# Window attention and a sticky mixture of experts: the last eviction of an arm behind the switch, eight raw weight buffers, routing lists at two steps per chunk

## The chip, the cores and the metric

The kernel runs on one core of a Trainium2 chip. Five engines work side by side, each through its own queue in order: TensorE (PE in the profile, its weight loads PEld), VectorE (DVE), ScalarE (ACT), GpSimd (POOL) and SyncE (SP), which issues most DMAs. The metric is the device time in microseconds; the median of several runs counts.

## What is computed

Attention with a window of 32 to each side and 32 global tokens, over 8 batches and 8 heads, gives 576 rows of 512 numbers per batch, 4608 rows in all. Each row is then given to one of eight experts: the expert of its largest logit, or, where a second gate says so, the expert of the row before.

```python
for b in range(B):
    prev_e = -1
    for s in range(S):
        fresh_e = int(np.argmax(logits[b, s]))
        if s == 0 or local_gate[b, s] < 0.5:
            e = fresh_e
        else:
            e = prev_e if prev_e >= 0 else fresh_e
        prev_e = e
        ...
        h = np.maximum(x[b, s] @ w1[e], 0.0)
        out[b, s] = p[e] * (h @ w2[e])
```

All products of the experts are made in three passes, on a high and a low part of each operand: high by high, low by high, high by low.

## The kernel before

**Attention first, then blocks of experts.** `Attn.run` works off 48 units of attention. Behind them come the blocks of `Moe.run`, each with the weights of one expert. Blocks 0 to 2 are *early* ones of 256 rows, taken from the first five batches alone, and the rest of the attention and of the routing is threaded between their matmuls. Blocks 3 to 10 are one per expert (*rem* in the code): what is left of its rows, at most 512, in one of ten arms of a `Switch`, by their number. Behind them stand up to 14 *full* blocks of 256 rows, each within an `If`; with these inputs three of them run.

**Within a block.** `mm1` multiplies by the first weight: eight steps (`fc`) of 12 matmuls; ACT takes the relu out of PSUM as the high part (`hh`), DVE the low part (`hl`). In the program's names the parts of later blocks lie in tiles called `wp` and `wq`. `mm2` multiplies by the second weight for one group of 128 rows: eight steps of three matmuls into one PSUM bank. `store` evicts that bank on ACT, scaled by the gate (`y`), and POOL scatters `y` to the output by an indirect DMA. POOL also gathers the rows of coming blocks (`gather`, into `xr` and `xa`), and `xpose` turns them on PE, ACT and DVE.

**The arms.** `arm` chooses: case 0 (`half`), which has only a group of 128 rows (group 2) and turns its relu on PE; case 1 (group 3 alone beside it); cases 2 to 9, `part`, with groups 0, 1 and, over 384 rows, 3. Behind the switch `close` does group 2 for every arm; ahead of that PE, ACT and the others load the next condition (`cnd`) and give a hint for the next switch (`hint`). Instructions behind a switch that depend on an engine's work within an arm wait for the end of that engine's arm, because the ten arms are merged there.

**Weights.** SP loads 512 KB pieces into `raw`, four buffers used in turn. `split` casts a piece on ACT to its high part; `flush` lets DVE subtract it for the low part, and only then issues the next load into that buffer. Split pieces lie in a ring of nine, so that about one block is split ahead. When a split stands in the program is written out: `SP` for the early blocks, `step` for the others.

**Routing lists.** Each `hook`, one per `fc` in the early blocks, advances the generator `tail` by one `yield`. `tail` ends the attention, ranks the rows, and runs `lists`: `place` counts, `low` builds one-hot tiles (`o`), and `pick` forms its operands on DVE in `xT` and then sums on PE, in 34 small matmuls, the row numbers `idx` that the first rem block gathers by. `kinds` computes the conditions `cnd` of the switches. `rest` picks the remaining lists, in twelve larger steps and 34 matmuls more. In `early`, block 2 forces what is not yet done: `finish(True)` at the first step of its second group runs `tail` up to `LISTS` and issues the gathers, and the hint for the first switch follows.

Of the kernel before, what the change touches and what calls it, by code (L numbers as in the profile page):

```python
# [37 lines left out]
GCH = [1, 4, 7, 10, 13, 14]  # L38
NX = 3
LISTS = "lists"  # L40
HEAVY = "heavy"
NF = (B * S) // 256
NR = NF - NX - 1
# [55 lines left out]
class Attn:  # L99
# [422 lines left out]
    def tail(self, sg, sl, fin, rt, moe):  # L522
        b = B - 1
        fin = [x for x in fin if x[0] is not None]
        self.g_t(sg)
        yield
        self.g_av(sg)
        self.at2.close()
        moe.alloc_a()
        yield  # L530
        self.l_t(sl, 0)
        self.l_t(sl, 1)
        yield
        self.l_av(sl, 0)
        yield
        self.l_av(sl, 1)
        self.at1.close()
        moe.alloc_b()
        yield
        while fin:  # L540
            f, a = fin.pop(0)
            f(*a)
            yield
        self.f1g(b)
        yield
        self.f1(b, 3)
        yield
        self.f2g(b)
        yield
        self.f2(b)  # L550
        yield from lag(2)
        self.f3(b, rt, False)
        yield
        c = self.cur[b]
        yield from every(rt.keys(b, c["L"]), 2)
        yield
        yield from rt.stage_b(self.ps_t, self.ps_o, rt.probs(b, c["L"], c["xa"]))
        self.f4(b, rt)
        yield from rt.lists(self.ps_o)
        yield LISTS  # L560
        yield from every(rt.rest(self.ps_o), RE)


# [23 lines left out]
class Route:  # L587
# [414 lines left out]
    def lists(self, po):  # L1002
# [28 lines left out]
            yield from self.low(c0, min(c0 + 5, NT))  # L1031
        self.pk = (cid, phi)
        yield from self.pick(cid, phi, self.o2, 0, 4, 2 * NX, ((0, NT),), po)
        yield from self.kinds()
        nc.vector.tensor_scalar(out=self.eid[:, 0:NR], in0=self.ek[0:1], scalar1=float(E - 1), scalar2=None, op0=ALU.min)
        yield
        nc.vector.tensor_tensor(out=self.eoh[:, NX + E:NSLOT], in0=ge[:, :, 0:E], in1=ge[:, :, 1:E + 1], op=ALU.subtract)
        yield

    def kinds(self):  # L1040
        nc = self.nc
        nc.vector.tensor_scalar(out=self.cnd[:, 0:1], in0=self.lim[0:1, E - 1:E], scalar1=0.5, scalar2=float(-E), op0=ALU.mult, op1=ALU.add)
        yield
        q = self.tmp("kq", [1, E], I32)
# [23 lines left out]
class Moe:  # L1068
    def __init__(self, tc, cst, rt, xs, buf, raw, ps, w1, w2, out):
# [15 lines left out]
        self.xt0 = None  # L1085
        self.go = False
        self.got = False
        self.cv = {}
        self.tail = None
        self.raws, self.wp, self.pend, self.nld, self.ex = [], [], [], 0, {}  # L1090
# [153 lines left out]
    def hook(self, i, k):  # L1244
        if self.tail is not None:
            try:
                if next(self.tail) == LISTS:
                    self.go = True
            except StopIteration:
                self.tail = None  # L1250
        self.flush()
        if i == NX - 1:
            self.finish()
        for _ in range(SP[i][k]):
            self.split()

    def finish(self, force=False):
        while force and not self.go:
            self.go = next(self.tail) == LISTS
        if self.go and not self.got:  # L1260
            self.gather(NX)
            self.got = True
# [10 lines left out]
    def early(self, i):  # L1273
# [9 lines left out]
        for fc in range(8):  # L1283
            self.mm2(i, py, fc, 0, *x[2:])
            self.hook(i, 8 + fc)
            if not mid and fc in (1, 3):
                self.xpose(i + 1, fc // 2)
                if fc == 3 and i + 2 < NX:
                    self.gather(i + 2)
        self.store(py, 0)  # L1290
        py = self.py()
        if mid:
            self.widen()
        for fc in range(8):
            if mid and fc == 0:
                self.finish(True)
                self.hint(i + 1)
            self.mm2(i, py, fc, 1, *x[2:])
            self.hook(i, 16 + fc)
            if mid and fc in XPM:  # L1300
                self.xpose(i + 1, XPM.index(fc))
        self.store(py, 1)
        if mid:
            all_(self.tail or ())
            self.tail = None
            self.gather(i + 2)
            self.ph.t.append(self.ps[6])
            self.py.t.append(self.ps[7])

    def half(self, i):  # L1310
        nc = self.nc
        XH, XL, HH, HL = self.XH, self.XL, self.HH, self.HL
        hr = []
        js = slice(P * REM, P * REM + P)

        def turn(k):
            tp = self.xtp().rearrange("p (t k) -> p t k", k=P)[:, 0:2]
# [24 lines left out]

    def part(self, i, n0, n1, groups):
        x = self.XH, self.XL, self.HH, self.HL
        for fc in range(8):
            self.mm1(i, fc, *x, n0, n1)
            self.step(fc % 2 == 0)
        for g, j in enumerate(groups):
            py = self.py()
            for fc in range(8):  # L1350
                self.mm2(i, py, fc, j, *x[2:])
                if g == 0:
                    self.step(fc in (1, 4))
                    if fc in (2, 5):
                        self.xpose(i + 1, fc // 3)
            self.store(py, j)

    def close(self, i, j):
        py = self.py()
        for fc in range(8):  # L1360
            self.mm2(i, py, fc, j, self.HH, self.HL)
            self.step(fc in (1, 4))
# [6 lines left out]
    def arm(self, i, case):  # L1369
        if case == 0:  # L1370
            self.half(i)
        elif case == 1:
            self.part(i, 256, 512, [3])
        else:
            n = 256 + GRAIN * (case - 1)
            self.part(i, 0, n, [0, 1] + [3] * (n > 384))

    def bound(self, k, most):
        if k not in self.cv:
# [52 lines left out]
def kernel(ctx: ExitStack, tc: tile.TileContext, qk, qg, vw, wgl, wgg, w1, w2, out):  # L1432
# [17 lines left out]
    moe.hr = Ring([at.gsb[:, 0:256], at.gsb[:, 256:512]])  # L1450
    w = 2 * (2 * E + NR)
    rt.o2 = at.xT.rearrange("p a b -> p (a b)").bitcast(BF16)[:, 0:NT * 2 * w].rearrange("p (t a w) -> p t a w", a=2, w=w)
    moe.xr += [at.xa.t[0][:, k] for k in range(2)]
    at.at1, at.at2 = s1, s2
    at.run(rt, moe)
# [57 lines left out]
```

## Time and profile before

| | us |
|---|---|
| runs | 727.65, 728.07, 733.19 |
| median | 728.07 |
| profiled execution | 730.23 |
| its span, first to last instruction | 728.5 |
| attention with the first early block begun | 0 to about 255 |
| first arm starts | 331.91 |
| short arm (`half`) of the second rem block | 378 to 393 |
| first full block | 639.53 |
| last instruction on PE ends | 709.8 |

A group's row gives engine, line, busy time and count, and then the idle time just before its instructions with what ended it. In a timeline a number in brackets is the idle time before the row and behind the arrow what ended it; "issue" stands where the profile shows no releaser. The granted clock of PE was 0.974 on average.

### The profile page before, as it was taken

How to read it: one execution, taken by the hardware profiler on the slowest of the kernel's cores; microseconds unless marked ns; L12 is line 12 of the kernel's file. 1: busy time of each engine (PE TensorE's matmuls, PEld its weight loads, DVE VectorE, ACT ScalarE, POOL GpSimd, SP SyncE). 2: the span in 40 equal slices, each digit the busy share in tenths (PEclk: the TensorE clock that was granted, in tenths of full speed). 3: DMA queues.
4: the chain of work that ended last, by engine and by line, in shares of the span. 5: the costliest groups of instructions: out<-in, count | busy, mean ns of one | idle time of the engine just before them, and what ended most of it. 6: DMA issues, size and time to landing. Idle time of an engine off the chain costs nothing.

```text
span 728.5 us, 18458 instructions
## 1 busy us (share of the span) xinstructions
PE 678.0 (93%) x7253; PEld 562.8 (77%) x7253; DVE 435.5 (60%) x1141; ACT 344.8 (47%) x613; POOL 194.0 (27%) x320
## 2 busy tenths in 40 slices
PE   8999999999899899979996999989899999999990
PEld 6777777777667869958884979878788879799880
DVE  7878778778787777974427444335444425165560
ACT  4555555554445646623344534244444425255550
POOL 7534434434143110122042112140303030112210
PEclk9999999999999999989997999999999999999995
DMA  8866786866584677863437635445555533367762
GB/s 337 351 249 238 305 292 247 317 251 241 186 315 163 209 239 236 278 227 107 161 116 250 193 125 188 145 152 183 163 176 170 160 105 116 118 211 239 233 203 92
DMA packets 42789, 150.93 MB, mean 207 GB/s; under 512 B 7869, under 2 KB 9149, under 8 KB 38464
## 3 DMA queue, kind: packets, MB, share of 16 engines
q1 hardware_dynamic: 35392, 126.39, 50.1%
q0 software_dynamic: 6880, 21.90, 8.8%
q8 instruction: 77, 1.26, 0.7%
q14 instruction: 152, 1.25, 0.5%
q10 hardware_dynamic: 288, 0.13, 0.1%
HBM read 130.02 MB, written 19.42 MB: 205 GB/s over the span
## 4 chain that ended last, share of the span: by engine, by line
PE 31%; issue 20%; DVE 5%; POOL 3%; DMA 3%; ACT 1%; POOLq 0%; SPq 0%; ACTq 0%; DVEq 0%
PE ps L1233 15%; PE ps L1222 12%; DMA raw<-in_w_dram 2%; DVE wp L1148 2%; PE ps L1187 2%; POOL out_dram L1239 2%; POOL xr L1173 1%; PE ps L1330 1%; DVE wq L1148 1%; DMA xr<-xs,idx 1%; ACT y L1238 0%; DVE hl L1225 0%; ACT wp L1139 0%; DVE o L902 0%; DVE wp L1190 0%
## 5 line engine op out<-in xcount | busy, mean ns | idle before, releaser
L1233 PE MATMUL ps<-wp,wq 128*128 128x512 f32 x504 | 129.7, 404 | 4.6 <-ACT y L1238 3.2
L1148 DVE TENSOR_TENSOR wp<-raw,wp 128x1024 fp32r<-128x1024 f32 x79 | 95.6, 1219 | 61.4 <-ACT wp L1139 61.4
L1239 POOL DMA_INDIRECT out_dram<-y,tk x38 | 39.3, 1034 | 307.7 <-ACT y L1238 295.1
L1233 PEld LDWEIGHTS ps<-wp,wq 128*128 128x128 f32 x504 | 93.4, 190 | 26.5 <-ACT y L1238 4.9
L1222 PE MATMUL ps<-wp,wp 128*128 128x256 f32 (+5 forms) x672 | 109.7, 323 | 2.3 <-issue 2.3
L1222 PEld LDWEIGHTS ps<-wp,wp 128*128 128x128 f32 x672 | 103.5, 188 | 8.0 <-issue 3.0
L1139 ACT CAST wp<-raw 128x1024 fp32r<-128x1024 f32 x81 | 84.7, 1046 | 26.6 <-PE ps L1187 9.2
L1225 DVE SCALAR_TENSOR_TENSOR wq<-ps,wq 128x256 fp32r<-128x256 f32 (+5 forms) x80 | 41.6, 526 | 90.4 <-ACT wq L1224 81.0
L1224 ACT ACTIVATE wq<-ps 128x256 fp32r<-128x256 f32 (+5 forms) x80 | 37.1, 468 | 85.2 <-PE ps L1222 81.3
L190 POOL TENSOR_SCALAR_AFFINE_SELECT qbd<-raw 64x512 f32<-64x512 f32 x62 | 44.6, 720 | 120.4 <-PE ps L242 102.2
L242 PE MATMUL ps<-kx,qbd 128*64 128x128 f32 x1024 | 71.0, 279 | 2.9 <-issue 2.1
L242 PEld LDWEIGHTS ps<-kx,qbd 128*64 128x64 f32 x1024 | 54.7, 136 | 12.7 <-issue 7.4
L1238 ACT ACTIVATE y<-ps,pp 128x512 f32<-128x512 f32 x38 | 26.2, 688 | 76.2 <-PE ps L1233 73.9
L247 DVE TENSOR_REDUCE mx<-ps 128x4 f32<-128x512 f32 x64 | 43.9, 686 | 29.5 <-PE ps L242 29.3
L1173 POOL DMA_INDIRECT xr<-xs,idx x32 | 39.6, 1237 | 70.9 <-DVE L L390 17.5
L253 ACT ACTIVATE pe<-pe 128x512 f32<-128x512 f32 x64 | 40.7, 636 | 33.1 <-DVE pe L249 33.1
L249 DVE TENSOR_TENSOR pe<-ps,mx 128x512 f32<-128x512 f32 x64 | 44.0, 688 | 1.6
L275 PE MATMUL ps<-v,pt 128*32 128x65 f32 x2048 | 42.7, 222 | 2.0 <-DVE xa L283 0.8
L275 PEld LDWEIGHTS ps<-v,pt 128*32 128x32 f32 x2048 | 33.3, 110 | 13.8 <-issue 6.7
L190 POOL TENSOR_SCALAR_AFFINE_SELECT kx<-raw 128x384 f32<-128x384 f32 (+3 forms) x127 | 43.0, 372 | 3.4 <-DMA raw<-in_qk_dram 1.2
L261 ACT COPY pt<-ps 128x512 f32<-128x512 f32 x64 | 34.9, 610 | 16.5 <-PE ps L259 16.4
L1189 ACT CAST wp<-ps 128x512 fp32r<-128x512 f32 x40 | 23.4, 587 | 34.8 <-PE ps L1187 27.9
(270 smaller groups left out, 1117.9 us busy)
## 6 DMA issues: line engine op xcount, KB each, us to landing
raw<-in_w_dram SPq DMA_DIRECT2D x123, 512.0 KB, 3.5
v<-in_vw_dram SPq DMA_DIRECT2D x32, 1040.0 KB, 9.9
raw<-in_qk_dram SPq DMA_DIRECT2D x32, 528.0 KB, 6.3
xs<-xa SPq DMA_DIRECT2D x8, 1056.0 KB
qgb<-in_qg_dram SPq DMA_DIRECT2D x8, 128.0 KB, 3.2
out_dram<-y,tk POOLq DMA_INDIRECT x38, 2.7
xs<-xg SPq DMA_DIRECT2D x32, 16.0 KB, 4.1
xr<-xs,idx POOLq DMA_INDIRECT x32, 6.2
```

What stands on the lines that cost most here:

```text
L190: self.nc.gpsimd.affine_select(out=out, in_=in_, pattern=pat, compare_op=ALU.is_ge, fill=0.0, base=0, channel_multiplier=0)
L242: nc.tensor.matmul(sp[64 * t2:64 * t2 + 64, t], qbd[:, w], kf[:, f:f + P], start=False, stop=True, skip_group_check=True)
L247: nc.vector.tensor_reduce(out=mx, in_=st["sp"], axis=AX.X, op=ALU.max)
L249: nc.vector.tensor_tensor(out=st["pe"][:, 4 * hb:4 * hb + 4], in0=st["sp"], in1=mx.broadcast_to([P, 4, P]), op=ALU.subtract)
L275: nc.tensor.matmul(o[32 * w4:32 * w4 + 32, g, h], pt[:, 2 * g + w4 // 2, w4 % 2, h, :], v[:, w, h * (D + 1):(h + 1) * (D + 1)], start=True ...
L1139: nc.scalar.copy(out=hi, in_=raw)
L1148: (nc.gpsimd if pool else nc.vector).tensor_tensor(out=lo, in0=raw, in1=hi.bitcast(F32), op=ALU.subtract)
L1173: self.nc.gpsimd.indirect_dma_start(out=self.xr[j], out_offset=None, in_=src, in_offset=bass.IndirectOffsetOnAxis(ap=self.rt.idx[:, c0 + j ...
L1222: nc.tensor.matmul(ph, a[:, dc, fs], b_[:, dc, n0:n1], start=(n == 0), stop=(n == 11))
L1225: nc.vector.scalar_tensor_tensor(out=hl[:, fc, n0:n1], in0=ph, scalar=0.0, in1=hh[:, fc, n0:n1].bitcast(F32), op0=ALU.max, op1=ALU.subtract)
L1233: nc.tensor.matmul(py, a[:, fc, js], b_[:, fs], start=(fc == 0 and k == 0), stop=(fc == 7 and k == 2))
L1239: sc = nc.gpsimd.indirect_dma_start(out=self.out, out_offset=bass.IndirectOffsetOnAxis(ap=self.g[1][:, j:j + 1], axis=0), in_=y, in_offset ...
```

## The change

It has three parts.

1. *Eviction.* In the arms of a rem block the last group now goes to the PSUM bank `ps[7]`, and its `store` stands at the start of `close`, behind the switch, with the column 1 of the gates and row numbers. Over 384 rows the groups go in the order 3, 0, 1 instead of 0, 1, 3. Case 1 copies column 3 to column 1. `half`, which has no such group, sets the row numbers of column 1 to `1 << 20`, which the scatter drops. The other groups use banks 0 and 1 by number.
2. *Raw buffers.* After block 2 the ring `raw` takes four more buffers, in `xa` and `xT` of the attention, and four loads for them are issued at once.
3. *Lists.* `tail` now yields at every second step of `lists` and every third of `kinds`, which is a generator by itself with a mark `KINDS` behind it. In block 2 the gathers, if still missing, are issued before the first `store`; what is left of `kinds` is forced at the fifth step of the second group, and the first hint follows at its seventh.

```diff
@@ tail
-        yield from rt.lists(self.ps_o)
+        yield from every(rt.lists(self.ps_o), 2)
         yield LISTS
+        yield from every(rt.kinds(), 3)
+        yield KINDS
         yield from every(rt.rest(self.ps_o), RE)
@@ early
+        if mid:
+            self.widen()
+            self.finish(True)
         self.store(py, 0)
         py = self.py()
-        if mid:
-            self.widen()
         for fc in range(8):
-            if mid and fc == 0:
-                self.finish(True)
+            if mid and fc == 4:
+                while not self.known:
+                    self.take(next(self.tail))
+            if mid and fc == 6:
                 self.hint(i + 1)
...
+            self.py.k = 0
+            old = [self.raw() for _ in range(4)]
+            self.raw.t, self.raw.k = self.more + old, 0
+            for _ in self.more:
+                self.load()
@@ half
+        nc.vector.memset(self.g[1][:, 1:2], 1 << 20)
@@ part
         for g, j in enumerate(groups):
-            py = self.py()
+            last = j == groups[-1] and self.kind(i) == "rem"
+            py = self.ps[7] if last else self.py.t[g]
...
-            self.store(py, j)
+            if not last:
+                self.store(py, j)
@@ close
-        py = self.py()
+        py = self.py.t[j % 2]
+        if self.kind(i) == "rem":
+            self.store(self.ps[7], 1)
@@ arm
-            self.part(i, 0, n, [0, 1] + [3] * (n > 384))
+            self.part(i, 0, n, [3] * (n > 384) + [0, 1])
```

How this stands in the engines' queues, at the places that the prediction speaks of. First ACT at the end of the last arm and behind it; before, with `y2` as the eviction of the arm's last group from bank `ps7`:

```order
L1238 ACTIVATE y0_4316<-ps0_63,pp0_92 128x512
L1238 ACTIVATE y1_4317<-ps1_64,pp0_92 128x512
L1238 ACTIVATE y2_4318<-ps7_70,pp0_92 128x512
L1508 UNCONDITIONAL_BRANCH
L1380 TENSOR_LOAD cnd_296
L1386 SWITCH_STRIDE
L1386 ISA
L1386 BRANCH_PREFETCH_HINT
L1139 CAST wp6_4312<-raw1_78 128x1024
```

and now:

```order
L1242 ACTIVATE y0_4316<-ps0_63,pp0_92 128x512
L1242 ACTIVATE y1_4317<-ps1_64,pp0_92 128x512
L1532 UNCONDITIONAL_BRANCH
L1403 TENSOR_LOAD cnd_296
L1409 SWITCH_STRIDE
L1409 ISA
L1409 BRANCH_PREFETCH_HINT
L1242 ACTIVATE y2_4318<-ps7_70,pp0_92 128x512
L1143 CAST wp6_4312<-xT_112 128x1024
```

The eviction of `ps7` moved behind the branch, and the cast reads one of the new raw buffers.

PE around the 34 matmuls of the first `pick` (only its end is shown; `o1` and `xT` are its operands). Before, it stands in the first group of block 2 (bank `ps0`, weights `wq1`):

```order
L996 LDWEIGHTS o1_290
L996 MATMUL ps6_69<-xT_112,o1_290 128x8
L1233 MATMUL ps0_63<-wq1_4315,hh_90 128x512 x2
L1233 MATMUL ps0_63<-wq1_4315,hl_91 128x512
L1233 MATMUL ps0_63<-wq1_4315,hh_90 128x512 x2
```

and now in the second group of block 1 (bank `ps1`, with five of the eight steps still to come):

```order
L999 LDWEIGHTS o1_290
L999 MATMUL ps6_69<-xT_112,o1_290 128x8
L1237 MATMUL ps1_64<-wp1_101,hh_90 128x512 x2
L1237 MATMUL ps1_64<-wp1_101,hl_91 128x512
L1237 MATMUL ps1_64<-wp2_4207,hh_90 128x512 x2
```

`pick` moved up by 18 steps: five of that group, the eight of `mm1` and five of the first group of block 2.

DVE where the operands of that `pick` (`xT`) are made. Before, among the steps `hl` of block 2:

```order
L902 TENSOR_TENSOR o1_290<-io128_261,plo_289 128x384
L1225 SCALAR_TENSOR_TENSOR hl_91<-ps2_65,hh_90 128x256
L986 TENSOR_TENSOR xT_112<-cid_4745,phi_3669 128x34x4
L1148 TENSOR_TENSOR wp2_4207<-raw2_79,wp2_4207 128x1024
L1225 SCALAR_TENSOR_TENSOR hl_91<-ps3_66,hh_90 128x256
L988 TENSOR_TENSOR xT_112<-xT_112,t1_264 128x34x4
L990 TENSOR_SCALAR xT_112<-xT_112,ipf_266 128x34x4
```

and now ahead of all of them, between splits of weights that block 2 uses (`wq0`), the second of which is the one that starts at 295.68 us in the profile before:

```order
L1152 TENSOR_TENSOR wq0_4314<-raw0_77,wq0_4314 128x1024
L905 TENSOR_TENSOR o1_290<-io128_261,plo_289 128x384
L989 TENSOR_TENSOR xT_112<-cid_4700,phi_3669 128x34x4
L991 TENSOR_TENSOR xT_112<-xT_112,t1_264 128x34x4
L993 TENSOR_SCALAR xT_112<-xT_112,ipf_266 128x34x4
L1152 TENSOR_TENSOR wq0_4314<-raw1_78,wq0_4314 128x1024
L1001 TENSOR_SCALAR l1_3761<-ps6_69 128x4
```

The list steps moved ahead of the split of the second half of `wq0`, and the step that reads the result of `pick` follows right behind it.

More of the change, by code (lines that the diff above doesn't have):

```diff
@@ L40 @@
 LISTS = "lists"
+KINDS = "kinds"
 HEAVY = "heavy"
@@ L1033, in lists, with kinds @@
         yield from self.pick(cid, phi, self.o2, 0, 4, 2 * NX, ((0, NT),), po)
-        yield from self.kinds()
+    def kinds(self):
+        nc = self.nc
+        ge = self.ge[:, NX:]
         nc.vector.tensor_scalar(out=self.eid[:, 0:NR], in0=self.ek[0:1], scalar1=float(E - 1), scalar2=None, op0=ALU.min)
@@ L1038, in lists @@
         yield
-    def kinds(self):
-        nc = self.nc
         nc.vector.tensor_scalar(out=self.cnd[:, 0:1], in0=self.lim[0:1, E - 1:E], scalar1=0.5, scalar2=float(-E), op0=ALU.mult, op1=ALU.add)
@@ L1087, in __init__ @@
         self.got = False
+        self.known = False
         self.cv = {}
@@ L1246, in hook @@
             try:
-                if next(self.tail) == LISTS:
-                    self.go = True
+                self.take(next(self.tail))
             except StopIteration:
@@ L1255, in hook, with take @@
             self.split()
+    def take(self, v):
+        self.go = self.go or v == LISTS
+        self.known = self.known or v == KINDS
     def finish(self, force=False):
         while force and not self.go:
-            self.go = next(self.tail) == LISTS
+            self.take(next(self.tail))
         if self.go and not self.got:
@@ L1289, in early @@
                     self.gather(i + 2)
+        if mid:
+            self.widen()
+            self.finish(True)
         self.store(py, 0)
         py = self.py()
-        if mid:
-            self.widen()
         for fc in range(8):
-            if mid and fc == 0:
-                self.finish(True)
+            if mid and fc == 4:
+                while not self.known:
+                    self.take(next(self.tail))
+            if mid and fc == 6:
                 self.hint(i + 1)
@@ L1344, in part @@
         x = self.XH, self.XL, self.HH, self.HL
+        if groups == [3]:
+            for t in self.g:
+                self.nc.vector.tensor_copy(t[:, 1:2], t[:, 3:4])
         for fc in range(8):
@@ L1452 @@
     rt.o2 = at.xT.rearrange("p a b -> p (a b)").bitcast(BF16)[:, 0:NT * 2 * w].rearrange("p (t a w) -> p t a w", a=2, w=w)
+    moe.more = [at.xa.t[1].rearrange("p a b -> p (a b)")[:, 1056 * k:1056 * k + 1056] for k in range(2)] + [at.xT.rearrange("p a b -> p (a b)")[:, 1024 * k:1024 * k + 1024] for k in range(2)]
     moe.xr += [at.xa.t[0][:, k] for k in range(2)]
```

## The prediction

> **What bounds the kernel now.** I read the page first, then the waits of TensorE (PE) alone, then the timelines of each engine around each wait, then windows for the clock. PE is busy for nearly the whole span:
>
> ```profile
> span 728.5 us, 18458 instructions
> PE 678.0 (93%) x7253; PEld 562.8 (77%) x7253; DVE 435.5 (60%) x1141; ACT 344.8 (47%) x613; POOL 194.0 (27%) x320
> ```
>
> So a change can win only what PE waits for, or runs at a lower clock. What PE waited for in the expert phase, from 331 us to the end (us in total, times, longest):
>
> ```profile
> PE ps L1233 <- ACT y L1238: 5.6, 7, 0.8
> PE ps L1319 <- DVE wp L1190: 3.4, 1, 3.4
> PE ps L1222 <- issue: 2.3, 2, 1.4
> ```
>
> Three places matter: seven joins behind a switch (5.6 us), the one expert that takes the short arm `half`, and the early phase where the routing lists are made. The change has one part for each.
>
> **Part 1, the eviction behind the switch.** A join of the third expert, in the timelines of PE and ScalarE (ACT); columns are start, duration, engine, line:
>
> ```profile
> 422.50 7.18 PE L1233 MATMUL ps<-wp,wq 128*128 128x512 f32 x30
> 430.46 2.36 PE L1233 MATMUL ps<-wp,wq 128*128 128x512 f32 x9 [0.78 <-ACT y L1238]
> 429.72 0.69 ACT L1238 ACTIVATE y<-ps,pp 128x512 f32<-128x512 f32 x1 [4.85 <-PE ps L1233]
> ```
>
> PE ends the arm at 429.68, ACT evicts from 429.72 to 430.41, PE goes on at 430.46: the whole gap is the eviction. The bank that `close` fills first was evicted long before; the wait is for ACT's last instruction in the arm. With that eviction moved behind the switch, ACT's last instruction in the arm is the eviction of the group before, and the bracket says that ACT had been idle for 4.85 us; so the wait is met when PE arrives. What could be uncovered is the rest that stands there on PE: a branch, the load of the next condition and the hint. The nearest row where PE loads the same condition and takes a branch test is the step into the first full block:
>
> ```profile
> 639.53 11.51 PE L1222 MATMUL ps<-wp,wp 128*128 128x256 f32 x96
> ```
>
> Without a bracket behind it the row had no gap. Bounds per join are 0 and 0.8 us; I take nearly all, 5.5 us of 5.6. The eviction itself (0.69) now runs on ACT during `close`, and its DMA on the POOL queue goes just ahead of the next gathers; the rows that those gathers fetch are used a block later. In the arms with three groups the order 3, 0, 1 changes no count. The short arm gets one more eviction and a dropped scatter, under `close` as well: nothing.
>
> **Part 2, eight raw buffers.** In most blocks raw weights lie ready, so more of them change nothing. The exception is `half`, whose matmuls are so short that its six splits outrun four buffers. PE, ACT and VectorE (DVE) there:
>
> ```profile
> 387.11 0.81 PE L1187 MATMUL ps<-idf,xr 128*128 128x128 f32 x4 [0.81 <-DVE wq L1322]
> 391.29 0.69 PE L1319 MATMUL ps<-idf,gsb 128*128 128x128 f32 x2 [3.38 <-DVE wp L1190]
> 393.39 4.21 PE L1233 MATMUL ps<-wp,wq 128*128 128x512 f32 x9 [1.41 <-ACT wp L1139]
> ...
> 385.85 0.38 ACT L1321 CAST wq<-ps 128x256 fp32r<-128x256 f32 x1
> 388.98 1.04 ACT L1139 CAST wp<-raw 128x1024 fp32r<-128x1024 f32 x1 [2.75 <-DMA raw<-in_w_dram]
> ...
> 386.97 1.21 DVE L1148 TENSOR_TENSOR wp<-raw,wp 128x1024 fp32r<-128x1024 f32 x1
> 390.55 0.69 DVE L1190 TENSOR_TENSOR wp<-ps,wp 128x512 fp32r<-128x512 f32 x1 [2.36 <-ACT wp L1189]
> ```
>
> The cast at 388.98 waits 2.75 us for its DMA, and in ACT's queue the casts of the next rows stand behind it; DVE, then PE at 391.29, wait in turn. With eight buffers this raw piece was loaded a block earlier. The cast runs at 386.2, the ones behind it from 387.2 on, and DVE's step at 390.55 can start when its own split ends, 386.97 + 1.21 = 388.2, that is 2.4 us sooner, and all behind it shifts by 2.4. The PE gaps of 0.81 and 1.41 us have other causes and stay. So 2.4 us; the bounds are 0 (another wait steps in) and 5.6 (all three gaps). What is late next is the last split of the arm, which PE still awaits at the join.
>
> **Part 3, lists at two steps per chunk.** First what the old pace costs, PE and clock (windows: start, length, then busy PE, PEld, DVE, ACT, POOL, clock, DMA share, GB/s):
>
> ```profile
> 292.47 0.62 PE L1233 MATMUL ps<-wp,hh 128*128 128x512 f32 x2
> 300.86 1.21 PE L1222 MATMUL ps<-xh,wp 128*128 128x256 f32 x8 [0.48 <-issue]
> 308.05 0.63 PE L1233 MATMUL ps<-wq,hh 128*128 128x512 f32 x2
> 317.80 0.72 PE L1233 MATMUL ps<-wq,hh 128*128 128x512 f32 x2 [3.04 <-issue]
> 322.15 1.12 PE L1187 MATMUL ps<-idf,xr 128*128 128x128 f32 x4 [1.33 <-DMA xr<-xs,idx]
> 331.91 21.12 PE L1222 MATMUL ps<-wp,wp 128*128 128x480 f32 x96 [0.88 <-issue]
> ...
> 318.00:322.00 4.00, 2.82 (x9) 1.69 (x8) 3.06 (x6) 0.00 (x0) 3.08 (x4) 0.65 0.89 323
> 322.00:326.00 4.00, 3.85 (x12) 3.17 (x13) 2.04 (x6) 0.59 (x1) 0.17 (x1) 0.50 0.43 135
> 394.00:398.00 4.00, 4.00 (x14) 3.12 (x13) 1.69 (x2) 1.05 (x1) 1.78 (x2) 0.54 0.77 208
> ```
>
> The 3.04 us are PE's load of the switch condition, for which DVE must first finish the kinds; the 1.33 are the rows gathered too late. After the 3.04 the clock fell to 0.65 and 0.50, which lost 2.82 x 0.35 + 3.85 x 0.50 = 2.9 us. Together 0.48 + 3.04 + 1.33 + 2.9 = 7.8 us. With the new pace the lists and kinds are done within the second early block, and the rows are gathered before they are needed: all of this goes.
>
> But the matmuls of `pick` now stand in PE's queue in the second early block, after the third step of its second group, which PE reaches at 292.47, and DVE is not ready for them. DVE there (timeline, then the groups of 295.68 to 310.44):
>
> ```profile
> 285.85 0.43 DVE L1225 SCALAR_TENSOR_TENSOR hl<-ps,hh 128x256 fp32r<-128x256 f32 x1 [2.28 <-ACT hh L1224]
> 286.26 1.22 DVE L1148 TENSOR_TENSOR wp<-raw,wp 128x1024 fp32r<-128x1024 f32 x1
> 287.40 0.42 DVE L1225 SCALAR_TENSOR_TENSOR hl<-ps,hh 128x256 fp32r<-128x256 f32 x1
> 287.73 0.16 DVE L930 TENSOR_SCALAR mx<-left 128x8 f32<-128x8 f32 x1
> ...
> L1148 DVE TENSOR_TENSOR wq<-raw,wq 128x1024 fp32r<-128x1024 f32 x3 | 3.7, 1219 | 0.0
> L1148 DVE TENSOR_TENSOR wp<-raw,wp 128x1024 fp32r<-128x1024 f32 x3 | 3.7, 1219 | 0.0
> L1225 DVE SCALAR_TENSOR_TENSOR hl<-ps,hh 128x256 fp32r<-128x256 f32 x8 | 3.3, 418 | 1.0 <-ACT hh L1224 1.0
> ...
> 295.68 1.22 DVE L1148 TENSOR_TENSOR wq<-raw,wq 128x1024 fp32r<-128x1024 f32 x1
> 310.44 2.35 DVE L1148 TENSOR_TENSOR wp<-raw,wp 128x1024 fp32r<-128x1024 f32 x2
> ```
>
> The split that starts at 295.68 is, in the new order, the one that follows `pick`'s operands; in the old order those end only before 310.44. So all list steps of these 14.76 us now come ahead of 295.68. They are what is left when the six splits (start to start 287.40 - 286.26 = 1.14, so 6.8), the eight hl steps (287.73 - 287.40 = 0.33, so 2.6) and the 1.0 of idle time are taken off: 4.3 us. About 0.6 of it (five small steps like the 0.16 at 287.73) can slip under DVE's wait of 2.28 before 285.85; DVE has no other free time before 295.68. The operands are ready at 295.68 + 4.3 - 0.6 = 299.4, and PE stands from 292.47: 6.9 us. A clock drop follows; its price is the recovery once PE is busy again, by the window 394 to 398 some 4.00 x 0.46 = 1.8, with the 0.6 us before it 2.1. New loss 9.0 against the old 7.8: part 3 costs 1.2 us. Bounds: a gain of 7.8 if PE didn't stand there at all, and a loss of 7.7 if the third block also waits (rival 3). I stay with 1.2, since the DVE order is fixed and its rows have no gaps.
>
> In the third early block DVE gets the twelve remaining selection steps, 6.4 us (rows at rival 3), between the hl steps. PE asks for the last hl after eight steps of (308.05 - 300.86) / 5 = 1.44 us and seven of 0.7 (422.50: 30 matmuls, ten steps), 16.4 us into the block. DVE can start its first hl some 2.3 us in (one step, then ACT's eviction; an estimate); then come seven hl (2.3), the 6.4 and three splits (3.4), 14.4 us in all. Two microseconds of cover: I cost it at nothing, and without the cover it is rival 3. The hint for the first switch moves from before 317.80 to the seventh of the group's eight steps, two steps and the last `pick` ahead of the switch at 331.91. The later switches have one group between hint and switch, and of PE's issue waits at L1222 (2.3 us, two of them) one is the 0.88 at the first switch and one lies within an arm: no other switch shows any. So nothing, with bounds 0 and 5.8 (rival 4).
>
> On the clock, the Trainium skill's page TensorE: Matmul & The Clock Gate (Part 1: The HAM clock gate) gives about 3.4 us of sustained work until full rate returns. By that each recovery would cost 1.7 us rather than my 2.1, and the sum would be 0.4 us lower.
>
> **The sum.** -5.5 - 2.4 + 1.2 = -6.7 us. The profiled execution took 730.23 us (span 728.5), which becomes 723.5; it lies 2.2 above the median of the runs, 728.07, which becomes 721.4. Other waits of PE stay: they come from what ACT and DVE need after each switch,
>
> ```profile
> 486.30 0.46 ACT L1224 ACTIVATE wq<-ps 128x352 fp32r<-128x352 f32 x1 [3.83 <-PE ps L1222]
> 524.54 1.86 PE L1222 MATMUL ps<-wp,wp 128*128 128x288 f32 x12 [1.39 <-issue]
> SPq L1413 <- SPq L1413: 7.6, 2, 5.8
> ```
>
> where ACT's first eviction of an arm comes late although the matmuls it needs ended about 3 us before, and PE runs out of banks when the group is narrow (1.39). The last row is SyncE's own branch out of the blocks, 5.8 us, the longest branch I find.
>
> **The rivals.** (1) PE doesn't stand at `pick`: the lists then only gain, 728.07 - 5.5 - 2.4 - 7.8 = 712.4, or about 714.5 with one clock drop left. For it speaks only that the steps themselves are small; against it DVE's unbroken rows. (2) The join wait stays, because something else of the arm ends last, and the change does not do what it says: 721.4 + 5.5 = 726.9. Against it: in the order ACT's last row of the arm is an earlier eviction. (3) The slower side: DVE becomes the bound of the third early block. Its selection steps there are
>
> ```profile
> L988 DVE TENSOR_TENSOR xT<-xT,t 128x486 bf16<-128x486 bf16 (+1 forms) x4 | 2.5, 636 | 0.1
> L986 DVE TENSOR_TENSOR xT<-cid,phi 128x486 bf16<-128x486 bf16 (+1 forms) x4 | 2.5, 629 | 0.9 <-issue 0.9
> L990 DVE TENSOR_SCALAR xT<-xT,ipf 128x486 bf16<-128x486 bf16 (+1 forms) x4 | 1.4, 347 | 0.1
> ```
>
> 6.4 us, which the old order ran where DVE was half idle. If none is hidden PE is 6.5 us later, 727.9; with a second clock recovery, 2.1, 730.0. It decides against the change from 6.7 us of such waits on; against it speaks that PE's own stand lets DVE catch up. (4) The first switch finds PE without its code: +3.8 by ACT's row, +5.8 by SyncE's, 725.2 to 727.2. The Trainium skill's page Runtime: NRT & Kernel Launch (Instruction fetch mechanics) speaks for it: a taken branch out of the two pages held stops until the target is fetched. The trace agrees for ACT and DVE after a switch, not for PE.
>
> **How the numbers follow.** Chances: forecast as worked out 0.60, with its own range 718.5 to 725 from the clock and the half arm; rival 1 0.14; rival 2 0.08; rival 3 0.08; rival 4 0.10. The likeliest is 721.4. The range that leaves out no more than 2 in 10 runs from 715 to 727.5. About 1% is what a measurement can tell from no change, that is 720.8 and 735.4. Faster takes all of rival 1 and 0.26 of the forecast, 0.40; slower by over 1% needs rival 3 with more than priced, 0.04; within 1% 0.56.
>
> **What would show it.** The seven waits of PE on ACT's y gone or near 0; the cast in `half` without its wait for a DMA and PE's 3.38 near 1; a wait of PE of about 7 us on DVE before `pick` in the second early block, a clock below 1 behind it, no wait at the condition load, none on the gathered rows; PE's first arm starting about 1 us later than 331.91. Wrong would be: no stand at `pick`, waits of PE for hl in the third block, or a gap of several us ahead of the first arm.

## The result, and the profile after

The changed kernel takes 724.03 us (median of 16 runs, 722.47 to 730.04) against 727.7 of the kernel before on the same chip: a ratio of 0.9949, with a 95% interval of 0.9925 to 0.9972. That is 3.7 us less; 721.4 had been forecast. The profiled execution took 724.97 us, its span 723.2.

The changed kernel's line numbers are three or four higher, and sixteen higher in `half`: `mm1` is L1226, `mm2` L1237, the eviction L1242, the cast L1143, `pick` on PE L999 (L996 before). PE's waits from 331 us on:

```profile
PE ps L1226 <- issue: 3.1, 2, 2.9
PE ps L1226 <- DVE wq L1229: 2.4, 2, 1.5
PE ps L1191 <- DVE wq L1338: 1.9, 2, 1.1
PE ps L1237 <- ACT wp L1143: 1.4, 1, 1.4
PE ps L1335 <- DVE wp L1194: 0.8, 1, 0.8
```

The seven waits for ACT's y (5.6 us) are gone, and the short arm's 3.4 has become 0.8. At the top stands a wait of 2.9 us that was 0.88 before. PE's timeline from the lists to the first arm:

```profile
298.81 1.05 PE L999 MATMUL ps<-xT,o 128*128 128x8 bf16 x34 [6.70 <-DVE xT L993]
314.11 1.21 PE L1226 MATMUL ps<-xh,wp 128*128 128x256 f32 x8 [0.63 <-DVE hl L1229]
317.83 0.73 PE L1237 MATMUL ps<-wq,hh 128*128 128x512 f32 x2 [0.55 <-DVE hl L1229]
329.43 0.72 PE L1237 MATMUL ps<-wq,hh 128*128 128x512 f32 x2 [0.22 <-issue]
336.05 4.54 PE L1226 MATMUL ps<-wp,wp 128*128 128x480 f32 x13 [2.90 <-issue]
```

PE stands 6.70 us at `pick`; the waits for the switch condition and for the gathered rows are gone. New are three waits of together 1.4 us in the third early block and the 2.90 ahead of the first arm. The short arm, PE and then ACT's cast of the piece that was late:

```profile
382.58 1.58 PE L1346 MATMUL ps<-hl,wp 128*128 128x256 f32 x12
...
393.38 0.69 PE L1335 MATMUL ps<-idf,gsb 128*128 128x128 f32 x2 [0.77 <-DVE wp L1194]
395.48 3.82 PE L1237 MATMUL ps<-wp,wq 128*128 128x512 f32 x9 [1.41 <-ACT wp L1143]
```

```profile
389.90 1.10 ACT L1143 CAST wp<-xa 128x1024 fp32r<-128x1024 f32 x1
```

The cast, now from a buffer in xa, waits for no DMA, and the arm takes 395.48 - 382.58 = 12.9 us, where it took 393.39 - 377.97 = 15.4. The windows show the granted clock (third number from the end) behind both long waits:

```profile
294.00:298.00 4.00, 0.00 (x0) 0.00 (x0) 3.96 (x9) 2.16 (x4) 2.66 (x1) 0.79 0.44 151
298.00:302.00 4.00, 3.19 (x40) 2.71 (x40) 3.66 (x10) 1.00 (x1) 0.71 (x1) 0.50 0.81 271
302.00:306.00 4.00, 4.00 (x21) 3.45 (x20) 1.93 (x9) 0.69 (x1) 0.00 (x0) 0.86 0.81 273
337.25:340.66 3.41, 3.41 (x10) 2.84 (x9) 0.00 (x0) 0.43 (x1) 1.66 (x2) 0.50 0.95 323
```

The clock of a window is a mean; a narrow window, as the last row, shows that it stood at 0.50. The recovery behind `pick` costs 3.19 x 0.50 + 4.00 x 0.14 = 2.2 us, the one behind the switch 3.41 x 0.50 = 1.7.

For a comparison of all kernels the profiled spans are cut at two places that every trace has: PE's last wait of the attention (at 271.85 in the kernel before, 1.09 us for `pc`) and the start of the first arm. "Early" lies between the two, "arms" from there to the end. What comes ahead of the first place varies from trace to trace by up to 4.5 us and is not touched by the change. Each kernel has one trace, so small differences in the table carry no weight.

| kernel | ratio to before (95% interval) | early, us | arms, us | gap ahead of the first arm, us |
|---|---|---|---|---|
| before | 1 | 60.06 | 396.59 | 0.88 |
| changed | 0.9949 (0.9925 to 0.9972) | 65.04 | 387.15 | 2.90 |
| part 1 alone | 0.9884 (0.9851 to 0.9916) | 60.15 | 386.78 | 1.19 |
| part 2 alone | 1.0005 (0.9981 to 1.0029) | 62.59 | 396.55 | 0.51 |
| part 3 alone | 1.0040 (1.0015 to 1.0065) | 61.68 | 396.05 | 1.07 |
| parts 1 and 2 | 0.9883 (0.9852 to 0.9913) | 60.53 | 385.94 | none |
| parts 1 and 2, loads late | 0.9861 (0.9827 to 0.9896) | 60.15 | 385.93 | 0.69 |
| changed, hint early | 0.9946 (0.9924 to 0.9968) | 62.99 | 386.11 | 2.29 |
| changed, loads late | 0.9886 (0.9851 to 0.9922) | 61.62 | 386.79 | 0.29 |
| changed, only xT loads late | 0.9927 (0.9898 to 0.9956) | 63.25 | 389.16 | 3.05 |
| changed, only xa loads late | 0.9890 (0.9833 to 0.9948) | 61.94 | 385.68 | 0.38 |
| changed, loads late, pick late | 0.9862 (0.9826 to 0.9898) | 61.82 | 386.32 | none |
| the same, five subtractions on POOL | 0.9898 (0.9846 to 0.9951) | 62.14 | 385.66 | none |
| parts 1 and 2, loads late, five on POOL | 0.9886 (0.9839 to 0.9933) | 63.28 | 386.54 | 1.02 |

So the change wins 9.4 us in the arms (forecast 7.9) and loses 5.0 in the early part (forecast 1.2). The experiments ask why.

### The profile page after: what moved, and what is told of

Same layout as the page of the kernel before. It is cut to its first block, busy times and chain, and to the rows that moved or that the text cites. A ratio compares the mean times of both kernels' runs of the same rounds, so it can differ in the third digit from the quotient of the medians.

```text
span 723.2 us, 18483 instructions
## 1 busy us (share of the span) xinstructions
PE 675.5 (93%) x7253; PEld 563.5 (78%) x7253; DVE 436.8 (60%) x1142; ACT 345.6 (48%) x614; POOL 192.8 (27%) x321
## 3 DMA queue, kind: packets, MB, share of 16 engines
q8 instruction: 77, 1.26, 0.7%
## 4 chain that ended last, share of the span: by engine, by line
PE 32%; issue 22%; DVE 5%; POOL 3%; ACT 1%; SPq 1%; DMA 0%; POOLq 0%; ACTq 0%; DVEq 0%
PE ps L1237 16%; PE ps L1226 13%; POOL out_dram L1243 2%; PE ps L1191 1%; POOL xr L1177 1%; DVE wp L1152 1%; DVE wq L1152 1%; DMA raw<-in_w_dram 0%; SPq L417 0%; DVE wp L1194 0%; PE ps L999 0%; DVE hl L1229 0%; DVE hl L1152 0%; ACT wp L1143 0%; DVE o L905 0%
## 5 line engine op out<-in xcount | busy, mean ns | idle before, releaser
L1243 POOL DMA_INDIRECT out_dram<-y,tk x39 | 42.0, 1078 | 340.0 <-ACT y L1242 326.9
L1237 PE MATMUL ps<-wp,wq 128*128 128x512 f32 x504 | 128.4, 402 | 1.4 <-ACT wp L1143 1.4
L1226 PE MATMUL ps<-wp,wp 128*128 128x256 f32 (+5 forms) x672 | 111.1, 325 | 4.5 <-issue 2.9
L1226 PEld LDWEIGHTS ps<-wp,wp 128*128 128x128 f32 x672 | 104.8, 190 | 10.3 <-issue 3.5
L1237 PEld LDWEIGHTS ps<-wp,wq 128*128 128x128 f32 x504 | 93.5, 190 | 21.9 <-ACT wp L1143 1.8
L1242 ACT ACTIVATE y<-ps,pp 128x512 f32<-128x512 f32 x39 | 26.8, 688 | 85.7 <-PE ps L1237 83.9
L1152 DVE TENSOR_TENSOR wp<-raw,wp 128x1024 fp32r<-128x1024 f32 x47 | 57.0, 1216 | 0.0
L1143 ACT CAST wp<-raw 128x1024 fp32r<-128x1024 f32 x49 | 51.1, 1045 | 6.2 <-DMA raw<-in_w_dram 5.4
L1152 DVE TENSOR_TENSOR wp<-xT,wp 128x1024 fp32r<-128x1024 f32 x16 | 19.6, 1225 | 52.9 <-ACT wp L1143 52.9
L1177 POOL DMA_INDIRECT xr<-xs,idx x32 | 35.4, 1106 | 38.3 <-DVE L L391 17.5
```

Of the source, the lines that this page charges most:

```text
L1143: nc.scalar.copy(out=hi, in_=raw)
L1152: (nc.gpsimd if pool else nc.vector).tensor_tensor(out=lo, in0=raw, in1=hi.bitcast(F32), op=ALU.subtract)
L1177: self.nc.gpsimd.indirect_dma_start(out=self.xr[j], out_offset=None, in_=src, in_offset=bass.IndirectOffsetOnAxis(ap=self.rt.idx[:, c0 + j ...
L1226: nc.tensor.matmul(ph, a[:, dc, fs], b_[:, dc, n0:n1], start=(n == 0), stop=(n == 11))
L1237: nc.tensor.matmul(py, a[:, fc, js], b_[:, fs], start=(fc == 0 and k == 0), stop=(fc == 7 and k == 2))
L1243: sc = nc.gpsimd.indirect_dma_start(out=self.out, out_offset=bass.IndirectOffsetOnAxis(ap=self.g[1][:, j:j + 1], axis=0), in_=y, in_offset ...
```

## The experiments

**What widens the gap ahead of the first arm.** Two things moved there at once: the hint, from eight steps ahead of the switch to two (theory A), and the four extra raw loads of part 2 (theory B). Four kernels vary them apart.

Part 3 alone:

> Part 3 alone (lists at two steps per chunk, hint late), no extra raw buffers, eviction as before. The gap ahead of PE's first arm was 0.88 us in the kernel before and is 2.90 us in the changed kernel, with a clock of 0.67 behind it. Theory A (the hint comes too late before the switch): the gap stays near 2.9 us with a clock drop behind it, and the first arm starts some 4.8 us later than before, about 336.7 us. Theory B (the four extra raw loads, which are issued right ahead of the switch, slow the fetch of PE's code): the gap is near 0.9 us with no clock drop, and the first arm starts about 333 us. Under both the stand at pick is near 6.7 us. Joins wait as before (5.6 us in seven). Time: A 731 to 733 us, B 728.5 to 730 us, against 727.7 of the kernel before.

PE's timeline there:

```profile
296.60 1.05 PE L999 MATMUL ps<-xT,o 128*128 128x8 bf16 x34 [6.84 <-DVE xT L993]
330.35 14.84 PE L1226 MATMUL ps<-wp,wp 128*128 128x480 f32 x67 [1.07 <-issue]
```

The hint is as late as in the changed kernel, and the gap is 1.07 us with a clock of 1.00 behind it: theory B's picture. The median is 729.15 us.

Part 2 alone, the code of the diff's loads by itself:

```diff
             self.py.t.append(self.ps[7])
+            old = [self.raw() for _ in range(4)]
+            self.raw.t, self.raw.k = self.more + old, 0
+            for _ in self.more:
+                self.load()
```

> Part 2 alone (eight raw buffers, the four extra loads issued at the end of the third early block), lists, hint and eviction as before. Theory A (a late hint makes the gap): the gap ahead of PE's first arm stays near 0.9 us, the short arm loses its DMA wait (PE's 3.38 us becomes about 1), and the time is 2.4 us under the kernel before, 725.3 us. Theory B (the burst of loads makes the gap): the gap is near 2.9 us with a clock drop behind it, and the gain of the short arm is given back there: 727 to 729 us.

The gap is 0.51 us, as theory A had it, and the time, 728.41 us, is that of theory B. The run doesn't tell them apart, since the loads are issued elsewhere here. PE's timeline (three rows), then SP's queue:

```profile
320.08 1.11 PE L1187 MATMUL ps<-idf,xr 128*128 128x128 f32 x4 [4.20 <-DMA xr<-xs,idx]
330.15 15.06 PE L1222 MATMUL ps<-wp,wp 128*128 128x480 f32 x68 [0.51 <-issue]
387.12 0.69 PE L1323 MATMUL ps<-idf,gsb 128*128 128x128 f32 x2 [1.08 <-DVE wp L1190]
```

```profile
313.35 0.86 SPq L1129 DMA_DIRECT2D xa<-in_w_dram  x2
328.91 1.09 SPq L1129 DMA_DIRECT2D xT<-in_w_dram  x2
```

Without part 3 the two loads into the buffers of xa are issued at 313.35, long before the switch. There they run at the time of the gather of the first rows, for which PE then waits 4.20 us instead of 1.33. The short arm's wait falls from 3.38 to 1.08 as predicted, but the kernel is no faster: what the short arm wins is lost at the gather and in later waits of PE for DVE.

In the changed kernel SP issues those loads elsewhere:

```profile
301.42 25.15 SPq L1133 DMA_DIRECT2D raw<-in_w_dram  x9
327.65 0.85 SPq L1133 DMA_DIRECT2D xa<-in_w_dram  x2
332.42 1.10 SPq L1133 DMA_DIRECT2D xT<-in_w_dram  x2
```

Now the hint early, in the changed kernel:

```diff
-            if mid and fc == 4:
+            if mid and fc == 0:
                 while not self.known:
                     self.take(next(self.tail))
-            if mid and fc == 6:
                 self.hint(i + 1)
```

> The changed kernel with the kinds forced and the first hint given ahead of the first of the eight steps of the last early group, not at its seventh. Theory A (late hint): PE's gap ahead of the first arm falls from 2.90 to about 0.9 us and the clock behind it stays above 0.95, together 3.4 us, so 720.6 us against 724.0 of the changed kernel. Theory B (burst of loads): the gap stays near 2.9 us and the time near 724. Forcing the kinds earlier moves about four DVE steps ahead of the group; if DVE is short there (rival 3), waits for hl of 1 us or so take part of it.

```profile
332.19 13.12 PE L1226 MATMUL ps<-wp,wp 128*128 128x480 f32 x52 [2.29 <-issue]
```

The gap is 2.29 us, and the ratio of 0.9946 is that of the changed kernel: A falls. (The early part of the profiled execution is 2.0 us shorter, 0.6 of it the gap; over the runs no difference shows.) The counterpart leaves the hint and moves the loads, from the end of the third early block to the `close` of the first rem block:

```diff
-            old = [self.raw() for _ in range(4)]
-            self.raw.t, self.raw.k = self.more + old, 0
-            for _ in self.more:
-                self.load()
...
         if self.kind(i) == "rem":
             self.store(self.ps[7], 1)
+        if i == NX:
+            old = [self.raw() for _ in range(4)]
+            self.raw.t, self.raw.k = self.more + old, 0
+            for _ in self.more:
+                self.load()
```

> The changed kernel with the four extra raw loads issued in the close of the first block behind the switch, not right ahead of the switch; hint late as in the changed kernel. Theory A (late hint): the gap of 2.90 us ahead of PE's first arm and the clock drop behind it stay, and the time is near 724.0 us. Theory B (burst of loads): the gap falls to about 0.9 us and the clock stays above 0.95, so about 720.6 us. Under both the short arm, a block later, keeps its gain (PE's wait there below 1 us).

```profile
330.61 14.59 PE L1226 MATMUL ps<-wp,wp 128*128 128x480 f32 x66 [0.29 <-issue]
383.18 0.66 PE L1191 MATMUL ps<-idf,xr 128*128 128x128 f32 x4 [1.10 <-DVE wq L1334]
384.65 0.66 PE L1191 MATMUL ps<-idf,xr 128*128 128x128 f32 x4 [0.81 <-DVE wq L1334]
386.38 0.44 PE L1331 MATMUL ps<-idf,gsb 128*128 128x128 f32 x2 [1.08 <-DVE wp L1194]
```

The gap is 0.29, the early part 3.4 us shorter than in the changed kernel, and the median 719.0 us. The two intervals, 0.9851 to 0.9922 and 0.9925 to 0.9972, do not overlap.

What PE may be waiting for shows in the trace's DMA view. Code comes over queues of its own kind, "instruction"; q8 brings 77 packets of 16 KB in a run. Two rows of the view of 330 to 334 us of the changed kernel (queue, packets, MB, share of 16 engines); q1 carries SP's loads:

```profile
q1 hardware_dynamic: 328, 1.19, 83.9%
q8 instruction: 1, 0.02, 1.7%
```

and of 326 to 330 us of the kernel with late loads:

```profile
q1 hardware_dynamic: 87, 0.29, 17.9%
q8 instruction: 1, 0.02, 1.8%
```

The packet itself is no slower behind the loads (1.7% of 4 us on 16 engines are 1.1 us, and 1.8% are 1.2); it starts later. One q8 packet comes ahead of the first arm in every trace. Narrow windows of 0.1 us give the time at which it starts; the last `pick` on PE, 1.8 us long, is the work just ahead of the switch:

| kernel | last `pick` starts | packet | first arm starts | arm after packet |
|---|---|---|---|---|
| before | 329.24 | 328.9 | 331.91 | 3.0 |
| part 3 alone | 327.49 | 327.6 | 330.35 | 2.8 |
| part 2 alone | 327.86 | 327.1 | 330.15 | 3.0 |
| changed, loads late | 328.52 | 327.8 | 330.61 | 2.8 |
| changed | 331.36 | 333.3 | 336.05 | 2.8 |
| changed, hint early | 328.11 | 329.6 | 332.19 | 2.6 |

In the four kernels without loads into xa just ahead of the switch the packet comes between 0.8 us before and 0.1 after the start of `pick` (0.5 after in part 1 alone, whose gap is 1.19); behind the loads it comes 1.5 to 1.9 after it. The arm starts 2.6 to 3.0 us after its packet in all of them. That q8 is PE's own queue is inferred from this, not named by the trace; and whether the code is asked for late or waits behind the data, no view shows.

Two more kernels split the burst. With the changed kernel's loads into xa where they are and those into xT late:

> The changed kernel with the two loads into the buffers of xa where they are (issued at 327.65 us in its trace) and the two into xT, issued at 332.42, put off to the close of the first block. Theory B (the code packet, which lands at 333.3 us, queues behind transfers issued before it): the xT loads come too late to hold it up, so the gap ahead of the first arm stays above 2 us, and the time near 724 us. Rival (PE's gap comes from all four loads or from those into xT): the gap falls below 1 us and the time to about 719 to 720.

```profile
331.44 13.77 PE L1226 MATMUL ps<-wp,wp 128*128 128x480 f32 x50 [3.05 <-issue]
```

and the other way round:

> The changed kernel with the two loads into xT where they are and the two into the buffers of xa put off to the close of the first block. Theory B: the gap ahead of the first arm falls from 2.90 to below 1 us and no clock drop follows, so 719 to 720.5 us. Rival (the xT loads matter): the gap stays above 2 us, 723 to 724 us.

```profile
330.62 14.63 PE L1226 MATMUL ps<-wp,wp 128*128 128x480 f32 x66 [0.38 <-issue]
```

The two loads into xa alone make the gap, the two into xT do not: with the first the packet comes 2.2 us after `pick` starts (328.8 against 326.60), just as the loads run out (q1 has no packet from 329.5 us to the arm); with the second it comes 0.4 before (328.0 against 328.45). Theory B holds, down to which two transfers. (With the first, the clock stands at 0.50 for 6.8 us behind the gap, 5.75 of them busy, which costs 2.9 us: its arms are the longest of the kernels with part 1.) The medians, 722.31 and 719.71 us, agree with it, though their intervals overlap.

**What each part is worth alone.** Part 1 alone:

> Part 1 alone (eviction behind the switch), all else as before. Prediction: the seven waits of PE on ACT's y (5.6 us) go and nothing takes their place, so 5.5 us under the kernel before, 721.5 us. Rival: the blocks behind each join now wait elsewhere (for ACT, which has the eviction in front of its casts), and less than 3 us is gained: above 724 us.

It gives 719.0 us against 726.51, a ratio of 0.9884: 8.4 us with an interval of 6.1 to 10.8, more than the 5.5 forecast and more than all three parts together. One join, in the kernel before and then in the changed one; the row behind each is the transposes after nine matmuls of `close`:

```profile
422.50 7.18 PE L1233 MATMUL ps<-wp,wq 128*128 128x512 f32 x30
430.46 2.36 PE L1233 MATMUL ps<-wp,wq 128*128 128x512 f32 x9 [0.78 <-ACT y L1238]
432.65 0.60 PE L1187 MATMUL ps<-idf,xa 128*128 128x128 f32 x4
```

```profile
425.52 9.28 PE L1237 MATMUL ps<-wp,wq 128*128 128x512 f32 x39
434.63 0.60 PE L1191 MATMUL ps<-idf,xa 128*128 128x128 f32 x4
```

The same 39 matmuls took 432.65 - 422.50 = 10.15 us and take 434.63 - 425.52 = 9.11 without the wait: 1.04 us for this join, where the bracket says 0.78. The rest stands beside the bracket: the 30 matmuls take 7.18 us, where 30 steps of 9.11 / 39 are 7.01, and the nine take 432.65 - 430.46 = 2.19, where nine steps are 2.10. In the trace of part 1 alone the seven joins, measured over the same 19 matmuls each, save 1.04 to 1.10 us, together 7.5. The short arm's wait is also shorter there, without any more buffers:

```profile
384.58 0.69 PE L1321 MATMUL ps<-idf,gsb 128*128 128x128 f32 x2 [2.14 <-DVE wp L1190]
```

which is 1.2 less; the arm is 386.67 - 372.71 = 14.0 us long, 1.5 less than before. Why the raw piece comes sooner there was not tried. The block behind the short arm gives 0.7 back, mostly by a new wait of PE for DVE's wq (0.65), and 0.7 lies behind PE's last instruction, where the traces differ by up to 1.1. So of the 9.8 us that the arms gain, 7.5 + 1.5 - 0.7 + 0.7 = 9.0 are assigned and 0.8 are not.

Parts 1 and 2 without part 3:

> Parts 1 and 2 without part 3 (lists, kinds and hint as before; four extra loads at the end of the third early block). Theory C (the extra loads of xa, issued at once when they no longer stand behind the lists, collide with the gather of the first rows, which waited 4.2 us in the kernel with part 2 alone and 1.3 before): part 1 gains 5.5 us, part 2 gives its 2.4 us back at the gather, so 721.5 us. Prediction's rows alone (part 2 gains 2.4 wherever it stands): 719.1 us. The seven joins do not wait, and the first PE gap ahead of the arm is below 1 us under both.

718.32 us. That number is nearer to 719.1, but only because part 1 is worth more than both expectations gave it. Beside part 1 alone, timed on the same chip against the same runs, part 2 adds nothing (0.9883 and 0.9884); with its 2.4 us the ratio would be 0.985, at the lower end of the interval. The gather waits 2.58 us here, against 0.41 in part 1 alone and 4.20 in part 2 alone, as theory C says.

The same with the loads late:

> Parts 1 and 2 without part 3, the four extra raw loads issued in the close of the first block behind the switch. Theory C (the loads of part 2 cost what they collide with, and the short arm gains 2.4 us by itself): 727.0 - 5.5 - 2.4 = 719.1 us, with the wait for the gathered rows back near 1.3 us; part 3 is then worth nothing, since the changed kernel with late loads also has 719.0. Rival (part 2 gains nothing over the whole, since the blocks behind the short arm wait more): 721.5 us.

716.48 us. The gather's wait is back at 1.27 us, the short arm's is 1.08, and the arms are as in the run before. It is the best median of all and lies under the changed kernel's interval, but not under those of the other kernels with part 1. So by the ratios part 2 is worth nothing (loads early) or 1.7 us (loads late) once part 1 is there, and neither differs from the other beyond the intervals. The traces say where its 2.4 us stay. Part 2 alone takes the short arm from 15.4 to 389.21 - 376.24 = 13.0 us, but part 1 alone has it at 14.0 already, and with both it is 12.9: the buffers add 1.1. And in the block behind it PE then waits where it did not wait before, in the changed kernel

```profile
410.80 2.19 PE L1226 MATMUL ps<-wp,hl 128*128 128x352 f32 x12 [0.90 <-DVE wq L1229]
```

against 0.65 with part 1 alone. Part 3 shows no gain: with the loads late, the kernels with and without it differ by 0.0025, in favour of the one without, inside either interval.

**The stand at pick.** If only its place is wrong, it goes when the matmuls stand later in PE's queue. Here they stand 20 steps (ten chunks) behind their operands instead of two, with the loads late:

```diff
-        yield from self.pick(cid, phi, self.o2, 0, 4, 2 * NX, ((0, NT),), po)
+        yield from self.pick(cid, phi, self.o2, 0, 4, 2 * NX, ((0, NT),), po, 20)
```

> The changed kernel with late raw loads (719.0 us) and with the matmuls of the first pick ten chunks later in PE's queue, so that PE does not stand in front of operands that DVE has not made. Theory D (the stand is a matter of place alone): the stand of 6.6 us and the clock drop behind it (some 2 us) go to below 1 us together: 711 to 713 us. Rival (DVE is the bound of this stretch and only catches up while PE stands): PE waits for hl in the second and third early block instead, several waits of 0.5 to 1.5 us, and at most 3 us are gained: 716 to 719 us.

```profile
300.77 1.21 PE L1226 MATMUL ps<-xh,wp 128*128 128x256 f32 x8 [2.40 <-DVE hl L1229]
325.34 0.76 PE L1191 MATMUL ps<-idf,xa 128*128 128x128 f32 x4 [2.91 <-DVE wp L1194]
```

The stand is gone, and PE waits for DVE's hl and DVE's transposed rows instead, 2.40 and 2.91 us. The early part is 61.82 us long, against 61.62. Theory D falls. From 285 to 300 us DVE is busy for 14.8 of 15 us here, and ahead of the wait at 325 it has no gap either: DVE is the bound, and where PE waits for it is a matter of order.

**Less work for DVE.** If DVE is the bound, five weight subtractions moved to POOL should tell:

```diff
         for _ in range(SP[i][k]):
-            self.split()
+            self.split((i, k) in ((1, 1), (1, 5), (1, 11), (2, 1), (2, 5)))
```

> The kernel with late loads and late pick (718.2 us), with five of the weight subtractions of the second and third early blocks on POOL instead of DVE (five times 1.22 us of DVE's time; POOL takes 2.4 us for one and is nearly idle there). Theory E (DVE is the bound of the early blocks, so PE's waits there, 2.4 and 2.9 us, shrink with DVE's work): 3 to 6 us less, 712 to 715 us. Rival (POOL's slower subtractions come late for PE, or hold up POOL's evictions and gathers): new waits of PE on POOL's wp or on the gathered rows, 717 us or more.

719.53 us, and PE's wait for the transposed rows is 4.64 us rather than 2.91. In the kernel without part 3:

> Parts 1 and 2 with late loads and the old pace of the lists (716.5 us), with the same five subtractions on POOL. Theory E: the waits for the switch condition (3.0 us), the gathered rows (1.3) and hl (0.9) and the clock drop behind them come from a late DVE, so 3 to 6 us less: 710.5 to 713.5 us. Rival as in the run before: 716 us or more.

719.21 us; no gain either, and the early part is 3.1 us longer. The gain of theory E does not come, but the rival's waits (for POOL's wp) are not there. The timelines say what happened: POOL, then DVE, at the same place of this kernel,

```profile
297.80 2.41 POOL L1148 TENSOR_TENSOR wp<-raw,wp 128x1024 fp32r<-128x1024 f32 x1 [1.44 <-ACT wp L1139]
```

```profile
297.51 0.41 DVE L1225 SCALAR_TENSOR_TENSOR hl<-ps,hh 128x256 fp32r<-128x256 f32 x1
297.85 2.40 DVE L1023 SCALAR_TENSOR_TENSOR cid<-k,m 128x13 bf16<-128x13 f32 x1
```

and DVE in the same kernel without the moved subtractions:

```profile
297.43 0.17 DVE L1023 SCALAR_TENSOR_TENSOR cid<-k,m 128x13 bf16<-128x13 f32 x1
```

A step of 0.17 us took 2.40, until POOL had ended; the `hl` steps, which read PSUM, ran beside POOL (0.42 at 281.52). It is so five times; four of the steps have groups of their own among DVE's (the last number but one is the mean in ns):

```profile
L902 DVE TENSOR_TENSOR o<-io,plo 128x384 bf16<-128x384 bf16 x1 | 2.7, 2668 | 0.0
L1023 DVE SCALAR_TENSOR_TENSOR cid<-k,m 128x13 bf16<-128x13 f32 x1 | 2.4, 2405 | 0.0
L913 DVE TENSOR_SCALAR f<-cn 128x8 int32<-128x8 int32 x1 | 2.0, 2043 | 0.0
L927 DVE SCALAR_TENSOR_TENSOR left<-f,sp 128x8 f32<-128x8 int32 x1 | 1.8, 1841 | 0.0
```

Together they are 9.0 us; unblocked they take 0.55, 0.17, 0.16 and 0.16 us in the kernel without the moved subtractions, so 7.9 us are lost in four steps, more than the 6.1 (five times 1.22) that were moved away. The fifth, L1192, takes 2.20 instead of 0.16. In the first of the two kernels three of the five subtractions each hold a DVE step for 1.88 us or more (a scan of 128x8, L919, takes 2055 ns). So these two runs do not test whether less work on DVE would help; they gave it no less.

## Why the prediction came out near, and where it was wrong

The total came close (724.0 for 721.4) by luck: two errors went against each other, too little for part 1 and too little for what part 2 costs beside part 3.

- **Part 1: right in mechanism, too small.** The seven waits are gone and nothing took their place. The term took the bracket (0.8 a join) as the price of a wait; in the pitch of the matmuls a join cost 1.04 to 1.10. The bound of "0 and 0.8 us" a join was no upper bound.
- **Part 2: right in the short arm, wrong in the sum.** "2.4 us sooner" is what the arm shows (12.9 us long against 15.4, and 13.0 with part 2 alone), with the join's 1.41 next in line as said. As a gain for the kernel it was too much: part 1 by itself shortens the arm by 1.5, not all behind the arm shifts with it, since the next block then waits for DVE, and alone the part measured nothing.
- **The step that failed** is Part 2's sentence that in most blocks raw weights lie ready, so that more of them change nothing. It priced where the pieces are used, not where the four loads are issued. They are 2 MB in SP's queue, and they cost where PE waits for something else that they delay: the gather without part 3 (4.20 us for 1.33), the code ahead of the first arm with it (2.90 for 0.88). In the `close` of the first block they cost nothing that shows.
- **Part 3: right in size.** The stand of 6.9 us measured 6.70, its clock recovery 2.2 for 2.1, the old waits are gone. Alone it made the early part 1.6 us longer, for 1.2 forecast, and the kernel 1.1 to 4.7 us slower by the runs. "Two microseconds of cover" in the third block was too much: PE waits 1.2 us for `hl` there.
- **Rival 4 had the place, not the cause.** It put 3.8 to 5.8 us on a first switch that finds PE without its code. Without the gap the kernel is 4.6 us faster by the ratios (0.9949 and 0.9886), and 3.8 by the two traces: 3.4 in the early part and 0.4 in the arms, where the kernel with late loads loses elsewhere most of the 1.7 that it saves on the clock. But the hint's place, its cause in the prediction, changes little (a gap of 2.29 for 2.90): the packet comes late when the two loads into xa run ahead of it.
- **Rival 3** came in part: DVE does bound the early blocks, as the late `pick` shows, but it took 1.2 us there, not 6.5.
- **The sentence on the clock** has a slip in its sum. It takes 1.7 us for the new recovery alone; taken for the old one of 2.9 as well, the sum would be some 0.8 us higher, not 0.4 lower.

## What to carry to other kernels

A prefetch costs where its transfers run, not only where its data is used: after a change in buffers, look up in the trace where the queue issues the new loads, and what else needs the DMA engines then, code for the next branch included. A short wait of TensorE on an eviction was worth more here than its bracket says (1.04 to 1.10 us for 0.78 to 0.83), so measure it by the pitch of the same matmuls with and without it. And where DVE bounded a stretch, moving the place at which PE waits for it brought nothing here.

## What the runs showed of the hardware

A 16 KB packet of code started 1.5 to 2.2 us after the start of `pick` behind 1 MB of loads, and otherwise between 2.3 before and 0.5 after it; PE's next work started 2.5 to 3.0 us after the start of the packet in every trace with a gap there. The Trainium skill's page Runtime: NRT & Kernel Launch (Instruction fetch mechanics) has each sequencer fetch its code in blocks of 16 KiB over a DMA queue of its own; the packets agree (1.26 MB in 77). It does not say that they come late when data on other queues run ahead of them, which these runs show.

The clock fell to 0.50 behind waits shorter than the 3.38 us of the kernel before: for 3.41 us behind one of 2.90, and in the short arm of the kernel with late loads for 6.83 us from the third of three waits of 1.10, 0.81 and 1.08 on:

```profile
386.96:393.79 6.83, 5.57 (x15) 4.53 (x16) 3.38 (x8) 3.15 (x5) 0.97 (x1) 0.50 0.86 284
```

The Trainium skill's page TensorE: Matmul & The Clock Gate (Part 1: The HAM clock gate) has the clock fall after an idle window of about 3.4 us; here it fell with less.

A POOL subtraction of 2.4 us that reads two tensors held up one DVE step until it ended, five times out of five in one kernel (1.84 to 2.67 us for 0.16 to 0.55) and three out of five in the other. The Trainium skill's page SBUF — State Buffer (SBUF: two separate sides) calls the port that the two share an exclusive lock, held for a whole instruction; the steps that waited agree.
